# Decayed attention and two MLPs on one core: two heads' first score tiles put into one, and one read over two PSUM banks

## The chip, the core and the metric

The kernel runs on one core of a Trainium2 chip. TensorE (PE) multiplies matrices into PSUM; VectorE (DVE) and ScalarE (ACT) read PSUM and work on SBUF; GpSimd (POOL) fills and reduces small things; SyncE (SP) issues nearly all DMAs. The metric is the time of one execution in microseconds of the device, as the median of several.

## The reference

Four batches of eight heads, 576 positions, 64 features a head; then two MLPs over the 2304 tokens.

```python
scores = q @ k.T / 8
cum = cumsum(log(clip(f, 1e-4, 1)))            # f: batch, head, position
scores = where(causal, scores + cum_q - cum_k, -1e9)
attn = exp(scores - max); attn = attn / (sum(attn) + 1e-9)
x = (attn @ v)                                  # heads side by side: 2304 x 512
h = x @ w_in;  y = maximum(0.01 * h, h) @ w_out # 512 -> 2048 -> 512
g = y @ w_gate; out = (silu(g) * (y @ w_val)) @ w_out2   # 512 -> 1536 -> 512
```

All is fp32 outside. Inside, most products are taken as three half-precision products of high and low parts.

## The kernel before

**Units.** Each batch is cut into two units of queries (`UNITS`, L467): u = 0 has queries 0 to 319 (below: a 320-query unit), u = 1 queries 320 to 575 (a 256-query unit). The query tiles of 128 rows are shifted by half a tile (`hw` = 64), so that tile i holds queries 128 i - 64 to 128 i + 63. Tile 0 thus has 64 rows that nobody uses. `KW` (L469) has the width in keys of each tile: 128, 256 and 320 for u = 0, 448 and 576 for u = 1.

**Attention of a unit** (`attention`, L891). For each of four pairs of heads, and each head: `prep_head` (L721) loads q and k into `xf`, and makes `ta` and `tb` from it (rounded part, rest, and four rows of the decay, `cum`, that SP loads into `tb`); `ta` and `tb` have two buffers each. Then `exps` (L757) for each tile: two matmuls, from `tb` and `ta`, of at least 256 columns into a PSUM bank; `exp_of` (L744) with one VectorE instruction that scales, adds the mask, writes SBUF and takes the extreme of each row; and one exponential on ScalarE that sums the row too. The 576-key tile doesn't fit in a bank of 512 floats: it is two halves of 288 in two banks and two VectorE instructions, the second of which goes on from the first one's extreme. `probs` (L788) cuts the normalised tile into a high part (ScalarE) and a low part (VectorE) in `ph`, one DMA transposes both into `pt`, and some tiles later `pv` (L798) multiplies with V, two heads at a time on the two column halves of the array, and cuts the result into `xs_buf`. GpSimd clears the parts of `ph` that no tile writes. In batch 0 the scores need one matmul each; its 320-query unit has a form of its own (`attention_f32`, L820), which uses widths 64, 192 and 320 already.

**Work around it.** While a unit's attention runs, the first MLP (`moe_h`, `moe_y`) of the unit before is multiplied (`along`, L1350), which needs that unit's `xs_buf`. From the second unit of batch 1 on, `rate` (L1386) also spreads 36 places among the score tiles: `place` (L946) loads a block of second-MLP weights (512 KB, as 8-byte words), turns it into floats on VectorE, and stores it (256 KB). A last stage (`gate_val`, L1209, `out_stage`) does the second MLP over all tokens with Strassen-like products; three banks of `pp_ring` (L1148) serve a block.

**PSUM.** Eight banks: `ps_s` (three, scores), `ps_x` (one, PV), `ps_m` (four, first MLP); `ps_r`, `pp_ring` and `po_ring` use some of them again.

**Order.** Nothing runs as written: a `Plan` (L84) records all operations, estimates each duration (`cost`), draws an order for the five queues by lists with due times in 120 rounds and takes the one with the least simulated end (`emit`, L382). Each queue then runs its part in that order, and a waiting instruction holds what is behind it. All instructions so have the line of a helper, L415.

Of the kernel before, what the change touches and what calls it, by code (L numbers as in the profile page):

```python
# [9 lines left out]
F32 = mybir.dt.float32  # L10
# [11 lines left out]
P = 128  # L22
# [61 lines left out]
class Plan:  # L84
# [17 lines left out]
    def record(self, eng, method, args, kw):  # L102
        outs = [kw[k] for k in self.OUT if kw.get(k) is not None]
        ins = [x for k, x in kw.items() if k not in self.OUT and isinstance(x, bass.AP)]
        pos = [x for x in args if isinstance(x, bass.AP)]
        if pos and not kw.get("out"):
            outs.append(pos[0])
            pos = pos[1:]
        ins += pos
        dur, nbytes = self.cost(eng.name, method, outs, ins, self.pairs)  # L110
        fn = getattr(eng.real, method)
        if self.group is not None:
            op = self.group
            assert op.eng in (None, eng.name)
            op.eng = eng.name
            op.dur += dur
            op.calls.append((fn, args, kw))
        else:
            op = self.new(eng.name)
            op.dur = dur  # L120
            op.bytes = nbytes
            op.calls.append((fn, args, kw))
        op.reads += [(x.tensor.name,) + spans(x) for x in ins]

        op.writes += [(x.tensor.name,) + (spans(x) if x.space != PSUM else ((0, P), [(0, 2048)])) for x in outs]
        if self.group is None:
            self.close(op)
# [320 lines left out]
def body(ctx, tc, qk, v, f, w_in, w_out, w_gate, w_val, w_out2, out):  # L448
# [19 lines left out]
    KEYS = [q0 + nq for q0, nq, _ in UNITS]  # L468
    KW = [[max(i * P + hw, min(i + 1, 2) * P) for i in tiles] for _, _, tiles in UNITS]  # L469
    W = qk.shape[3]  # L470
# [22 lines left out]
    psp = ctx.enter_context(tc.tile_pool(name="ps", bufs=1, space=PSUM))  # L493
    banks = [psp.tile([P, 512], F32, name=f"bank{i}") for i in range(8)]
    ps_s, ps_x, ps_m, ps_r = Ring(banks[:3]), Ring(banks[3:4]), Ring(banks[4:]), Ring(banks[4:7])
    a_s = Arena(pool, 1856, "smalls")
# [18 lines left out]
    for u in range(2):  # L515
        a_m.at = n
        gf_ring[u] = a_m.cut(PER[u] * UNITS[u][1], F32, (5, 3)[u])
    raw_ring = a_w.cut(RAW * 2, I32, 3)
    cv_ring = a_w.cut(RAW, I32, 1)
# [105 lines left out]
    def decay():  # L625
# [26 lines left out]
        nc.gpsimd.affine_select(out=mask[:, 4 * P:], in_=mask[:, 4 * P:], pattern=[[-1, P + hw]],  # L652
                                compare_op=ALU.is_ge, fill=NEG, base=0, channel_multiplier=1)
        csf = scr[:, 3 * S:3 * S + 4 * W].rearrange("r (a s) -> r a s", a=4)
        cs = csf.bitcast(F32R)
# [87 lines left out]

    def exp_of(tp, parts, ms, mx, total):  # L744

        for n, (ps, a, e) in enumerate(parts):
            nc.vector.tensor_tensor_reduce(
                out=tp[:, a:e], in0=ps[:, :e - a], in1=ms[:, a:e], scale=-0.125,
                scalar=(3.0e38 if n == 0 else mx[:, 1:2]), op0=ALU.add, op1=ALU.min,
                accum_out=mx[:, 0:1] if n == len(parts) - 1 else mx[:, 1:2])  # L750
        w = parts[-1][2]
        nc.scalar.activation(out=tp[:, :w], in_=tp[:, :w], func=AF.Exp, bias=mx[:, 0:1], scale=-1.0, accum_out=total)

    def mask_of(i):
        return mask[:, (4 - i) * P + hw:]

    def exps(o, n):  # L757
# [3 lines left out]
        tp = tp_ring[o.u].next()  # L761
        mx = sm(2, "mx", 8)
        if kw <= 512:
            parts = [(0, kw, max(kw, 256))]
        else:
            parts = [(0, kw // 2, kw // 2), (kw // 2, kw, kw - kw // 2)]
        pss = []
        nc.begin()
        for a, e, w in parts:
            ps = ps_s.next()  # L770
            if o.b == 0:
                nc.tensor.matmul(ps[:, :w], lhsT=o.xf[:D + 2, q:q + P],
                                 rhs=o.xf[:D + 2, o.k.start + a:o.k.start + a + w], start=True, stop=True)
            for l in range(2 if o.b else 0):
                t, k = (o.tb, D + 4) if l == 0 else (o.ta, P)
                nc.tensor.matmul(ps[:, :w], lhsT=t[:k, q:q + P], rhs=t[:k, o.k.start + a:o.k.start + a + w],
                                 start=(l == 0), stop=(l == 1))
            pss.append(ps)
        nc.done()
        exp_of(tp, [(ps, a, e) for ps, (a, e, w) in zip(pss, parts)], mask_of(i), mx, o.sums[:, n:n + 1])  # L780
        o.tp.append((tp, kw))
        if n == len(KW[o.u]) - 1:
            nc.vector.tensor_scalar(out=o.sums[:, :n + 1], in0=o.sums[:, :n + 1], scalar1=1e-9, scalar2=1.0 / PSCALE,
                                    op0=ALU.add, op1=ALU.mult)
            o.rc = sm(3, "rc", 3)
            nc.vector.reciprocal(out=o.rc[:, :n + 1], in_=o.sums[:, :n + 1])

    def probs(g, n, hi, lo):  # L788

        tp, kw = g.tp[n]  # L790
        rc = g.rc[:, n:n + 1]
# [28 lines left out]
    def attention_f32():  # L820
# [9 lines left out]
        for h in range(H + 1):  # L830
            if h < H:
# [12 lines left out]
                for ci in tiles:  # L844
                    kw, q = KW0[ci], qc + ci * P - hw
                    ps, tp, mx = ps_s.next(), tp_ring[0].next(), sm(2, "mx", 8)
                    mms(ps[:, :kw], [(xf[:D + 2, q:q + P], xf[:D + 2, kc:kc + kw], True, True)])
                    exp_of(tp, [(ps, 0, kw)], mask_of(ci), mx, sums[:, ci:ci + 1])
                    tps.append(tp)
# [41 lines left out]
    def attention(b, u):  # L891

        later, t = [], 0
        nb = NBK[u] // 2
        at_block = [(5, 0, 2), (0, 4)][u]
        rests = [(4, 10), (3, 12)][u]
        for x in ph_ring.bufs if b else ():
            for i in rests:
                nc.gpsimd.memset(x[:, i * P + hw:(i + 1) * P], 0.0)
        for hp in range(NHP):  # L900
            pts = []
            for x in range(2):
                o = prep_head(b, u, 2 * hp + x)
                for n, kw in enumerate(KW[u]):
                    if later and later[0][0] <= t:
                        pv(*later.pop(0)[1])
                    exps(o, n)
                    t += 1
                    yield kw
                ph, pt = ph_ring.next(), pt_ring[u].next()  # L910
                for n, kw in enumerate(KW[u]):
                    hi, lo = (ph[:, (l * nb + at_block[n]) * P:][:, :kw] for l in range(2))
                    probs(o, n, hi, lo)
# [3 lines left out]
            def at(x, j, l, pts=pts):  # L917
                pb = blocks(pts[x])[:, l * nb:(l + 1) * nb, :]
                if u == 0:
                    if j == 2:  # L920
                        return [(pb[:, 4:5, hw:], 256)]
                    tail = [(pb[:, j:j + 3:2, :], hw)]
                    return tail if j else [(pb[:, 5:6, hw:], 0)] + tail
                if j == 4:
# [222 lines left out]
    s_o2, i_o2 = a_s.cut(1, F32), a_s.cut(1, F32)  # L1147
    pp_ring, po_ring = Ring(banks[:6]), Ring(banks[6:])  # L1148

# [235 lines left out]
    gv_places = chain(*(stage_gv(n) for n in range(NB2)), stage_o2())  # L1385
    rate = (4 * NB2 + NF2) / (sum(H * len(UNITS[u][2]) for _, u in todo) - 24)  # L1386
    for b, u in todo:
# [80 lines left out]
```

## Time and profile before

| | |
|---|---|
| median of three runs | 922.84 us (922.84 to 923.4) |
| profiled execution | 925.66 us, its span 923.9 us |
| mean granted TensorE clock | 0.998 |
| TensorE busy | 98% of the span |
| VectorE, ScalarE, GpSimd busy | 86%, 73%, 5% |

The span goes from the first to the last instruction of the profiled execution. The names on the left of an arrow are what an instruction writes, those on the right what it reads: `att_bytes` is the memory of the attention (`xf`, tiles, `ph`, `pt`), `wi_bytes` and `wo_bytes` that of weights, `moe_bytes` and `g_bytes` that of the first MLP, `smalls` holds numbers for each row, `bank` is PSUM. In the timeline, instructions of one kind that follow each other are one row, and "us" is from the first one's start to the last one's end; matmuls overlap.

### The profile page before, as it was taken

To read this page: it belongs to the slowest core of one execution; us is meant where nothing else is said; L and a number is where in the kernel's file an instruction comes from. 1 tells how busy PE (TensorE), PEld (TensorE's weight loads), DVE (VectorE), ACT (ScalarE), POOL (GpSimd) and SP (SyncE) were. 2 spreads that over 40 slices of the span, in tenths; PEclk is the share of its full clock that TensorE was granted. 3 is DMA by queue.
4 is the path that set the end of the run, shared out by engine and by line. 5 is a ranking of instruction groups with operands and counts; after the bars stand their busy time and mean duration, and the time that the engine had idled before them with its cause. 6 is when DMAs were issued, how large, how long until landed. Compare 5 with 4: busy or idle time off the path is not lost.

```text
span 923.9 us, 25387 instructions
## 1 busy us (share of the span) xinstructions
PE 908.8 (98%) x10018; PEld 776.7 (84%) x10018; DVE 794.1 (86%) x2078; ACT 676.1 (73%) x1665; POOL 45.4 (5%) x119
## 2 busy tenths in 40 slices
PE   9999999999999999899999999999999999999998
PEld 5666678877688777788778899999999999999997
DVE  7999999988899999799788999986778695968685
ACT  8886689988689887688886878774647474755553
POOL 3410000000000010000000000000000000000000
PEclk9999999999999999999999999999999999999999
DMA  7568985797999999989867452110101000100001
GB/s 229 179 202 217 271 212 115 187 248 172 259 270 259 255 263 229 298 249 254 188 147 191 140 178 96 64 59 20 37 18 31 25 25 25 37 25 2 26 6 42
DMA packets 163431, 132.81 MB, mean 144 GB/s; under 512 B 117432, under 2 KB 130752, under 8 KB 163280
## 3 DMA queue, kind: packets, MB, share of 16 engines
q1 hardware_dynamic: 163312, 131.20, 53.5%
q8 instruction: 78, 1.28, 0.6%
q14 instruction: 41, 0.34, 0.1%
HBM read 79.99 MB, written 22.83 MB: 111 GB/s over the span
## 4 chain that ended last, share of the span: by engine, by line
PE 58%; DVE 7%; DMA 3%; ACT 3%; issue 1%; POOL 0%; SPq 0%; ACTq 0%; DVEq 0%; POOLq 0%
PE bank L415 58%; DVE att_bytes L415 2%; DVE stage L415 1%; DVE wo_bytes L415 1%; ACT att_bytes L415 1%; DMA tb<-out_dram 1%; ACT moe_bytes L415 1%; DMA att_bytes<-att_bytes 1%; DVE smalls L415 1%; DVE wi_bytes L415 1%; DMA att_bytes<-in_qk_dram 1%; DMA gate_val_dram<-wo_bytes 1%; DVE g_bytes L415 1%; DVE tb L415 0%; DVE ta L415 0%
## 5 line engine op out<-in xcount | busy, mean ns | idle before, releaser
L415 PEld LDWEIGHTS <-att_bytes 128*128 128x128 f16 (+1 forms) x4062 | 233.8, 100 | 18.3 <-issue 14.7
L415 PEld LDWEIGHTS <-wi_bytes 128*128 128x128 f16 x2292 | 192.2, 98 | 42.4 <-issue 3.1
L415 PE MATMUL bank<-g_bytes,wo_bytes 128*128 128x256 f16 (+2 forms) x1472 | 209.7, 299 | 0.0
L415 PE MATMUL bank<-moe_bytes,wi_bytes 128*128 128x320 f16 (+1 forms) x1536 | 194.5, 286 | 1.5 <-ACT moe_bytes L415 1.5
L415 ACT ACTIVATE att_bytes<-att_bytes,smalls 128x320 f32<-128x320 f32 (+11 forms) x308 | 173.7, 591 | 30.1 <-DVE smalls L415 25.5
L415 PEld LDWEIGHTS <-wo_bytes 128*128 128x128 f16 x1344 | 128.1, 98 | 33.5 <-issue 1.8
L415 DVE TENSOR_TENSOR wi_bytes<-bank,wi_bytes 128x256 f32<-128x256 f32 x270 | 109.4, 418 | 45.0 <-PE bank L415 43.6
L415 PEld LDWEIGHTS <-g_bytes 128*128 128x128 f16 x1620 | 125.9, 98 | 9.0
L415 ACT ACTIVATE wi_bytes<-wi_bytes,smalls 128x256 f32<-128x256 f32 (+2 forms) x129 | 69.9, 555 | 44.9 <-DVE wi_bytes L415 42.4
L415 PE MATMUL bank<-wi_bytes,att_bytes 128*128 128x128 f16 x1680 | 98.7, 219 | 0.5 <-ACT wi_bytes L415 0.3
L415 DVE SCALAR_TENSOR_TENSOR att_bytes<-att_bytes,smalls 128x576 f16<-128x576 f32 (+5 forms) x148 | 86.8, 614 | 4.1 <-ACT att_bytes L415 3.7
L415 PE MATMUL bank<-stage,att_bytes 128*128 128x128 f16 (+1 forms) x1389 | 86.7, 221 | 0.6 <-DVE wi_bytes L415 0.6
L415 ACT COPY wi_bytes<-bank 128x256 f32<-128x256 f32 x108 | 38.4, 363 | 51.8 <-PE bank L415 47.6
L415 DVE CUSTOM_DVE_ANT_0 att_bytes<-bank,att_bytes 128x320 f32<-128x320 f32 (+5 forms) x160 | 67.7, 441 | 7.2 <-PE bank L415 7.1
L415 POOL PARTITION_ALL_REDUCE smalls<-smalls x54 | 28.2, 523 | 757.1 <-DVE smalls L415 718.3
L415 PE MATMUL bank<-att_bytes 128*64 128x256 f16 (+4 forms) x828 | 55.5, 262 | 5.5 <-DMA att_bytes<-att_bytes 5.2
L415 ACT ACTIVATE wi_bytes<-wo_bytes 128x256 bf16<-128x256 f32 x108 | 44.0, 410 | 19.2 <-DVE wo_bytes L415 19.2
L415 PE MATMUL bank<-wo_bytes,g_bytes 128*128 128x256 f16 x432 | 55.0, 273 | 0.0
L415 DVE TENSOR_TENSOR g_bytes<-moe_bytes,g_bytes 128x320 f16<-128x320 f32 (+1 forms) x80 | 44.6, 564 | 8.2 <-ACT g_bytes L415 7.8
L415 PE MATMUL bank<-tb 68*128 68x256 f32 (+3 forms) x144 | 49.9, 360 | 1.7 <-ACT att_bytes L415 1.1
L415 DVE SCALAR_TENSOR_TENSOR stage<-stage 128x512 int32<-128x512 int32 x68 | 46.5, 684 | 0.2
L415 DVE SCALAR_TENSOR_TENSOR wo_bytes<-wi_bytes,smalls 128x512 f32<-128x512 f32 x54 | 40.1, 743 | 6.3 <-ACT wi_bytes L415 6.3
(123 smaller groups left out, 1380.1 us busy)
## 6 DMA issues: line engine op xcount, KB each, us to landing
stage<-in_moe_w_out_dram SPq DMA_DIRECT2D x28, 512.0 KB
att_bytes<-in_qk_dram SPq DMA_DIRECT2D x24, 416.0 KB
stage<-in_moe_w_in_dram SPq DMA_DIRECT2D x16, 512.0 KB
att_bytes<-in_qk_dram SPq DMA_DIRECT2D x24, 320.0 KB
stage<-in_moe_w_gate_dram SPq DMA_DIRECT2D x12, 512.0 KB
stage<-in_moe_w_val_dram SPq DMA_DIRECT2D x12, 512.0 KB
stage<-gate_val_dram SPq DMA_DIRECT2D x12, 512.0 KB
ta<-y_dram SPq DMA_DIRECT2D x18, 256.0 KB
```

The costliest lines, as they stand in the source:

```text
L415: fn(*args, **kw)
```

## The change

The first score tiles of a pair of heads share one tile of 64 keys: `exps_two` puts queries 0 to 63 of the one head on PSUM rows 0 to 63 and those of the other on rows 64 to 127, with four fp32 matmuls of 64 columns, two terms for each head, on the two column halves. It runs when the second head is prepared; its probabilities go into the second head's `ph`, and the first head's transpose has 10 blocks in place of 12. The second tiles are 192 keys wide, with matmuls of 256 columns as before. The 576-key tile lies in `two`, a tile over two banks, 288 columns on either side of the border, and one VectorE instruction reads it. A 320-query unit has 20 score tiles for 24. The banks are dealt anew: scores of a unit alternate between one bank and `two`; the last stage has five product banks for six. `rate` is worked out from the smaller number of tiles.

```diff
-        op.reads += [(x.tensor.name,) + spans(x) for x in ins]
-        op.writes += [(x.tensor.name,) + (spans(x) if x.space != PSUM else ((0, P), [(0, 2048)])) for x in outs]
+        bank = (0, P), [(0, 4096)]
+        op.reads += [(x.tensor.name,) + (spans(x) if x.space != PSUM else bank) for x in ins]
+        op.writes += [(x.tensor.name,) + (spans(x) if x.space != PSUM else bank) for x in outs]
...
-    KW = [[max(i * P + hw, min(i + 1, 2) * P) for i in tiles] for _, _, tiles in UNITS]
+    KW = [[i * P + hw for i in tiles] for _, _, tiles in UNITS]
...
-    banks = [psp.tile([P, 512], F32, name=f"bank{i}") for i in range(8)]
-    ps_s, ps_x, ps_m, ps_r = Ring(banks[:3]), Ring(banks[3:4]), Ring(banks[4:]), Ring(banks[4:7])
+    banks = [psp.tile([P, 512], F32, name=f"bank{i}") for i in range(6)]
+    two = psp.tile([P, 2 * 512], F32, name="banks")
+    ps_x, ps_m, ps_r = Ring(banks[1:2]), Ring(banks[2:]), Ring(banks[1:4])
+    ps_s, ps_f = Ring([banks[0], two]), Ring([banks[0], two, banks[4]])
...
+    mask2 = a_s.cut(hw, BF16)
...
+        for x in range(2):
+            r = slice(x * hw, (x + 1) * hw)
+            nc.scalar.copy(out=mask2[r, :], in_=mask[r, 4 * P + x * hw:4 * P + (x + 1) * hw])
...
-    def exp_of(tp, parts, ms, mx, total):
-        for n, (ps, a, e) in enumerate(parts):
-            nc.vector.tensor_tensor_reduce(
-                out=tp[:, a:e], in0=ps[:, :e - a], in1=ms[:, a:e], scale=-0.125,
-                scalar=(3.0e38 if n == 0 else mx[:, 1:2]), op0=ALU.add, op1=ALU.min,
-                accum_out=mx[:, 0:1] if n == len(parts) - 1 else mx[:, 1:2])
-        w = parts[-1][2]
-        nc.scalar.activation(out=tp[:, :w], in_=tp[:, :w], func=AF.Exp, bias=mx[:, 0:1], scale=-1.0, accum_out=total)
+    def exp_of(tp, ps, ms, mx, total):
+        nc.vector.tensor_tensor_reduce(out=tp, in0=ps, in1=ms[:, :tp.shape[1]], scale=-0.125, scalar=3.0e38,
+                                       op0=ALU.add, op1=ALU.min, accum_out=mx)
+        nc.scalar.activation(out=tp, in_=tp, func=AF.Exp, bias=mx, scale=-1.0, accum_out=total)
...
+    def exps_two(two):
+        b, kw = two[1], KW[0][0]
+        ps, tp, mx = ps_s.next(), tp_ring[0].next(), sm(1, "mx", 8)
+        nc.begin()
+        nc.pairs = True
+        for l in range(2):
+            for x, e in enumerate(two):
+                t, k = (e.tb, D + 4) if l == 0 else (e.ta, P)
+                t = t.bitcast(F32)
+                nc.tensor.matmul(ps[x * hw:(x + 1) * hw, :kw], lhsT=t[:k, e.q.start:e.q.start + hw],
+                                 rhs=t[:k, e.k.start:e.k.start + kw], start=(l == 0), stop=(l == 1))
+        nc.done()
+        nc.pairs = False
+        exp_of(tp[:, :kw], ps[:, :kw], mask2, mx, b.sums[:, :1])
+        b.tp.append((tp, kw))
...
-        mx = sm(2, "mx", 8)
-        if kw <= 512:
-            parts = [(0, kw, max(kw, 256))]
-        else:
-            parts = [(0, kw // 2, kw // 2), (kw // 2, kw, kw - kw // 2)]
-        pss = []
+        mx = sm(1, "mx", 8)
+        to = two if kw > 512 else ps_s.next()
+        if kw > 512:
+            ps_s.n += 1
+            assert ps_s.n % 2 == 0
+        c = 0 if kw <= 512 else 512 - kw // 2
         nc.begin()
-        for a, e, w in parts:
-            ps = ps_s.next()
+        for a, w in ((0, max(kw, 256)),) if kw <= 512 else ((0, kw // 2), (kw // 2, kw // 2)):
+            ps = to[:, c + a:]
...
-        exp_of(tp, [(ps, a, e) for ps, (a, e, w) in zip(pss, parts)], mask_of(i), mx, o.sums[:, n:n + 1])
+        exp_of(tp[:, :kw], to[:, c:c + kw], mask_of(i), mx, o.sums[:, n:n + 1])
         o.tp.append((tp, kw))
         if n == len(KW[o.u]) - 1:
...
-        tp, kw = g.tp[n]
+        tp, kw = g.tp[n - len(KW[g.u])]
...
-                    ps, tp, mx = ps_s.next(), tp_ring[0].next(), sm(2, "mx", 8)
+                    ps, tp, mx = ps_f.next(), tp_ring[0].next(), sm(1, "mx", 8)
...
-        nb = NBK[u] // 2
         at_block = [(5, 0, 2), (0, 4)][u]
-        rests = [(4, 10), (3, 12)][u]
-        for x in ph_ring.bufs if b else ():
+        nbs = [(5, 6), (9, 9)][u]
+        rests = [(4, 1, 5), (3,)][u]
+        assert ph_ring.n % 2 == 0
+        for x, nb in zip(ph_ring.bufs, nbs) if b else ():
             for i in rests:
-                nc.gpsimd.memset(x[:, i * P + hw:(i + 1) * P], 0.0)
+                for l in range(2) if i < nb else ():
+                    nc.gpsimd.memset(x[:, (l * nb + i) * P + hw:(l * nb + i + 1) * P], 0.0)
         for hp in range(NHP):
-            pts = []
+            pts, os = [], []
             for x in range(2):
                 o = prep_head(b, u, 2 * hp + x)
+                os.append(o)
+                nb, skip = nbs[x], (u, x) == (0, 0)
                 for n, kw in enumerate(KW[u]):
+                    if n == 0 and skip:
+                        continue
                     if later and later[0][0] <= t:
                         pv(*later.pop(0)[1])
-                    exps(o, n)
+                    if n == 0 and u == 0:
+                        exps_two(os)
+                        kw = 2 * kw
+                    else:
+                        exps(o, n)
                     t += 1
                     yield kw
...
-                pb = blocks(pts[x])[:, l * nb:(l + 1) * nb, :]
+                pb = blocks(pts[x])[:, l * nbs[x]:(l + 1) * nbs[x], :]
                 if u == 0:
                     if j == 2:
                         return [(pb[:, 4:5, hw:], 256)]
                     tail = [(pb[:, j:j + 3:2, :], hw)]
-                    return tail if j else [(pb[:, 5:6, hw:], 0)] + tail
+                    p0 = blocks(pts[1])[:, l * nbs[1] + 5:l * nbs[1] + 6, x * hw:(x + 1) * hw]
+                    return tail if j else [(p0, 0)] + tail
...
-    pp_ring, po_ring = Ring(banks[:6]), Ring(banks[6:])
+    pp_ring, po_ring = Ring(banks[:4] + [two[:, :512]]), Ring(banks[4:])
...
-    rate = (4 * NB2 + NF2) / (sum(H * len(UNITS[u][2]) for _, u in todo) - 24)
+    rate = (4 * NB2 + NF2) / (sum(H * len(UNITS[u][2]) - (0 if u else NHP) for _, u in todo) - 24)
```

## Rows read from the trace of the kernel before

**Rows 1.** The page, part 1: busy us (share of the span) xinstructions.

```profile
PE 908.8 (98%) x10018; PEld 776.7 (84%) x10018; DVE 794.1 (86%) x2078; ACT 676.1 (73%) x1665; POOL 45.4 (5%) x119
```

**Rows 2.** Waits of TensorE, whole span: us in total, times, longest us.

```profile
PE bank L415 <- DMA att_bytes<-att_bytes: 5.2, 3, 2.3
...
PE bank L415 <- ACT moe_bytes L415: 1.5, 3, 0.7
PE bank L415 <- ACT att_bytes L415: 1.1, 1, 1.1
PE bank L415 <- DVE smalls L415: 0.8, 2, 0.5
```

**Rows 3.** Windows: a 320-query unit, a 256-query unit, the last stage.

```profile
core 0: us, PE busy (x) PEld busy (x) DVE busy (x) ACT busy (x) POOL busy (x), PEclk, DMA share, GB/s
120.00:188.00 68.00, 66.88 (x637) 57.57 (x636) 64.28 (x194) 63.07 (x156) 3.65 (x12) 1.00 0.72 173
188.00:253.00 65.00, 63.38 (x523) 46.85 (x523) 56.64 (x164) 50.41 (x117) 3.98 (x13) 1.00 0.92 222
575.00:924.00 349.00, 345.76 (x5106) 332.59 (x5105) 267.84 (x578) 204.17 (x525) 6.39 (x15) 1.00 0.09 29
```

**Rows 4.** Timeline of TensorE at three unit ends: start, us, [idle before].

```profile
110.64 1.06 PE L415 MATMUL bank<-att_bytes 128*64 128x256 f16 x16 [1.26 <-DMA att_bytes<-att_bytes]
...
252.31 0.95 PE L415 MATMUL bank<-att_bytes 128*64 128x256 f16 x14 [1.62 <-DMA att_bytes<-att_bytes]
...
374.68 1.63 PE L415 MATMUL bank<-att_bytes 128*64 128x256 f16 x24 [2.35 <-DMA att_bytes<-att_bytes]
```

**Rows 5.** Window behind the third unit end, columns as in rows 3.

```profile
374.70:380.00 5.30, 5.30 (x46) 3.98 (x46) 3.53 (x14) 4.10 (x12) 0.32 (x3) 0.68 1.00 312
```

**Rows 6.** Timeline of TensorE around single tiles of first scores.

```profile
151.58 4.11 PE L415 MATMUL bank<-moe_bytes,wi_bytes 128*128 128x256 f16 x36
...
155.65 0.28 PE L415 MATMUL bank<-ta 128*128 128x256 f32 x1
155.77 1.48 PE L415 MATMUL bank<-g_bytes,wo_bytes 128*128 128x256 f16 x12
...
157.33 0.39 PE L415 MATMUL bank<-g_bytes,wo_bytes 128*128 128x256 f16 x2
```

**Rows 7.** Timeline of TensorE, matmuls on halves of the array.

```profile
45.84 0.33 PE L415 MATMUL bank<-att_bytes,g_bytes 64*64 64x64 f32 x4
...
46.10 0.64 PE L415 MATMUL bank<-att_bytes 66*128 66x448 f32 x1
...
146.34 0.93 PE L415 MATMUL bank<-moe_bytes,wi_bytes 128*128 128x256 f16 x7
147.19 0.33 PE L415 MATMUL bank<-att_bytes 128*64 128x64 f16 x4
```

**Rows 8.** Groups by form, VectorE: busy us, mean ns | idle.

```profile
L415 DVE CUSTOM_DVE_ANT_0 att_bytes<-bank,att_bytes 128x448 f32<-128x448 f32 x32 | 19.7, 615 | 1.6 <-PE bank L415 1.6
...
L415 DVE CUSTOM_DVE_ANT_0 att_bytes<-bank,att_bytes,smalls 128x288 f32<-128x288 f32 x32 | 16.4, 511 | 0.5
...
L415 DVE DVE_READ_ACCUMULATOR2_ANT smalls<- 128x1 f32 x192 | 15.4, 80 | 0.0
...
L415 DVE CUSTOM_DVE_ANT_0 att_bytes<-bank,att_bytes 128x288 f32<-128x288 f32 x32 | 14.4, 449 | 1.1 <-PE bank L415 1.0
...
L415 DVE SCALAR_TENSOR_TENSOR att_bytes<-att_bytes,smalls 128x128 f16<-128x128 f32 x24 | 8.2, 341 | 0.0
...
L415 DVE CUSTOM_DVE_ANT_0 att_bytes<-bank,att_bytes 128x128 f32<-128x128 f32 x24 | 6.6, 277 | 1.1 <-PE bank L415 1.1
```

**Rows 9.** Groups by form, ScalarE's exponentials, columns as in rows 8.

```profile
L415 ACT ACTIVATE att_bytes<-att_bytes,smalls 128x128 f32<-128x128 f32 x24 | 9.5, 397 | 4.1 <-DVE smalls L415 4.0
...
L415 ACT ACTIVATE att_bytes<-att_bytes,smalls 128x64 f32<-128x64 f32 x8 | 2.7, 338 | 0.0
```

**Rows 10.** SP: `cum` loads (min/median/max ns), and a transpose on the timeline.

```profile
L415 SPq DMA_DIRECT2D tb<-cum_dram x48: 261/283/1254, 100.9 to 470.0; - x48
...
367.68 4.80 SPq L415 DMA_TRANSPOSE att_bytes<-att_bytes  x1
```

More of the change, by code (lines that the diff above doesn't have):

```diff
@@ L777, in exps @@
                                  start=(l == 0), stop=(l == 1))
-            pss.append(ps)
         nc.done()
-        exp_of(tp, [(ps, a, e) for ps, (a, e, w) in zip(pss, parts)], mask_of(i), mx, o.sums[:, n:n + 1])
+        exp_of(tp[:, :kw], to[:, c:c + kw], mask_of(i), mx, o.sums[:, n:n + 1])
         o.tp.append((tp, kw))
         if n == len(KW[o.u]) - 1:
-            nc.vector.tensor_scalar(out=o.sums[:, :n + 1], in0=o.sums[:, :n + 1], scalar1=1e-9, scalar2=1.0 / PSCALE,
+            m = n + 1 - len(o.tp)
+            nc.vector.tensor_scalar(out=o.sums[:, m:n + 1], in0=o.sums[:, m:n + 1], scalar1=1e-9, scalar2=1.0 / PSCALE,
                                     op0=ALU.add, op1=ALU.mult)
             o.rc = sm(3, "rc", 3)
-            nc.vector.reciprocal(out=o.rc[:, :n + 1], in_=o.sums[:, :n + 1])
+            nc.vector.reciprocal(out=o.rc[:, m:n + 1], in_=o.sums[:, m:n + 1])
     def probs(g, n, hi, lo):
-        tp, kw = g.tp[n]
+        tp, kw = g.tp[n - len(KW[g.u])]
         rc = g.rc[:, n:n + 1]
@@ L845, in attention_f32 @@
                     kw, q = KW0[ci], qc + ci * P - hw
-                    ps, tp, mx = ps_s.next(), tp_ring[0].next(), sm(2, "mx", 8)
+                    ps, tp, mx = ps_f.next(), tp_ring[0].next(), sm(1, "mx", 8)
                     mms(ps[:, :kw], [(xf[:D + 2, q:q + P], xf[:D + 2, kc:kc + kw], True, True)])
-                    exp_of(tp, [(ps, 0, kw)], mask_of(ci), mx, sums[:, ci:ci + 1])
+                    exp_of(tp[:, :kw], ps[:, :kw], mask_of(ci), mx, sums[:, ci:ci + 1])
                     tps.append(tp)
@@ L911, in attention @@
                 for n, kw in enumerate(KW[u]):
+                    if n == 0 and skip:
+                        continue
                     hi, lo = (ph[:, (l * nb + at_block[n]) * P:][:, :kw] for l in range(2))
```

## The prediction

> **What bounds the kernel now.** First the page: TensorE is busy 908.8 of 923.9 us, VectorE 794.1, ScalarE 676.1 [rows 1]. So TensorE is the bound, and the change can gain in two ways only: shorter TensorE work, or fewer TensorE waits. The view of the waits, for TensorE alone, shows how little the second can be: 5.2 us for transposed probabilities (three waits), 1.5 for ScalarE's `moe_bytes` (the attention output cut for the next matmuls), 1.1 for ScalarE's `att_bytes`, 0.8 for VectorE [rows 2], 8.6 in all. The windows show why these waits stand in the attention: while the 320-query unit of batch 1 runs, VectorE is busy 64.28 of 68 us, in the 256-query unit after it 56.64 of 65; in the last stage, without attention, TensorE works 345.76 of 349 us [rows 3]. The three waits for transposes all close a 256-query unit, those of batches 0, 1 and 2: 1.26, 1.62 and 2.35 us [rows 4]. After the longest the granted clock is 0.68 over 5.3 us (partly at the lower of the two levels, 1.2 GHz); that lost another 5.3 x 0.32 = 1.7 us [rows 5]. In reach of the change, outside TensorE's own work, are thus 8.6 + 1.7 = 10.3 us.
>
> **TensorE's own work.** Before, a pair of heads has two tiles of first scores, each two matmuls of 256 columns (`max(kw, 256)` in `exps`). 36 half-precision matmuls and one such tile take 155.77 - 151.58 = 4.19 us, 12 and one tile 157.33 - 155.77 = 1.56 [rows 6]; the difference gives 0.1096 a matmul, and so 0.245 a tile, 0.49 a pair. After, it is four fp32 matmuls of 64 columns, two by two on halves of the array. The nearest row is the end of an fp32 PV group: four 64-column matmuls on halves, 46.10 - 45.84 = 0.26 with the way back to full width; the way in is 147.19 - (146.34 + 7 x 0.1096) = 0.08 [rows 7]. 0.34 in place of 0.49 for 12 pairs (batches 1 to 3): -1.8 us. Bounds: without the way in 0.26 (-2.8 us); if the halves do not overlap, since the new contraction is 68 and 128 rows and not 64, 0.08 + 2 x 0.26 = 0.60 (+1.3 us).
>
> A rule speaks against this part. A full-width matmul of 256 columns takes 0.28 us where the next starts 0.12 us later [rows 6], so about 0.16 is still in flight. The Trainium skill (TensorEngine Tiling (Array Packing), Key Properties) says that a change of tiling mode drains the engine. A whole drain on the way in would make a pair 0.26 + 0.16 = 0.42 and this part -0.8 us in place of -1.8; the sum below would be 918.8, inside the forecast's own range, and I give it a tenth of the forecast's chance. The trace has 0.08 for the way in, half of that drain, and I take the row.
>
> The 192-key tiles still have 256 matmul columns, the 576-key tiles still two matmuls of 288 for each term, and PV has as many matmuls of the same sizes: nothing.
>
> **VectorE and ScalarE.** A score read costs 615 ns for 448 columns, 449 for 288, hence 1.04 a column, and 80 for the accumulator read behind it [rows 8]. Nothing in the trace reads over two banks. Extrapolated, 576 columns take 615 + 128 x 1.04 = 748, and with 80 it is 0.83 us against 449 + 511 + 160 = 1.12: 0.29 less a tile. Bounds: none of it (the second bank costs what the second instruction did), or 0.29 + the 0.06 between 511 and 449. I take 0.29: one start, one accumulator read and one pointer fewer. For 32 tiles 9.3 us, 2.3 a 256-query unit. In a pair of first tiles two reads of 277 + 80 become one of 277 - 66 + 80 = 291: 0.42; two low parts of 341 become one of 275: 0.41; the 192-key tiles save 64 columns in two reads and two low parts: 0.27. Together 1.1 a pair, 4.4 a 320-query unit, 13.2 in three. ScalarE's exponentials go from two of 397 to one of 338 [rows 9], and its high parts and accumulator reads fall likewise: by estimate over 1 us a pair. VectorE's 64.28 of 68 us becomes about 59.9, 88% for 95%.
>
> None of this is on the path by itself; it counts where a chain of attention ends late. The 256-query units get part back: `rate` goes from 36/72 to 36/64, so that batches 1 and 2 stage 9 and not 8 weight places in such a unit. One place (`place`, for the gate and value weights) moves 512 KB in and 256 KB out; at the 222 GB/s of that stretch [rows 3] 3.5 us of transfers. There I count the gain in VectorE and the place against each other. Batch 0's unit has no places and keeps its 2.3 us, more than the 1.26 that it waits.
>
> So I let go: the waits for ScalarE and VectorE, 1.5 + 1.1 + 0.8 = 3.4 [rows 2], and the 1.26 of batch 0's end. The other two waits for transposes and the clock's 1.7 stay.
>
> **What the change adds.** The shared tile needs both heads' `ta` and `tb`, two buffers each. So the first head's are held until the second is prepared, and between the shared tile and the next pair stand two score tiles, not three. Then SP must load the `cum` rows into `tb` (median 0.28 us of issue, longest 1.25), behind transposes that hold SP up to 4.80 us [rows 10]. If the load comes late, the score matmul waits at the head of TensorE's queue, and every matmul behind it. First scores and 192- and 320-key tiles also have two PSUM places in turn, not three. Bounds for both together: nothing, or the 0.5 us of the longest wait for VectorE [rows 2] in each of 12 pairs, 6 us. I take a quarter, 1.5: a pair has 68 / 4 = 17 us [rows 3], and the median issue is far from the longest.
>
> At nothing: GpSimd clears 42 pieces and not 24, but it is busy 45.4 us in all [rows 1]; two small ScalarE copies for `mask2` lie in the start; half of 24 transposes have 10 blocks and not 12, too little on a queue that waits in order. The last stage has five product banks for six: each block takes three, and the third is the one its neighbour finished with two products earlier; TensorE's 345.76 of 349 us leave no wait to grow. If that cover were gone, a wait for ScalarE's copy would come in up to 54 blocks.
>
> **Sum.** -1.8 - 3.4 - 1.3 + 1.5 = -5.0 us. The profiled execution took 925.66 us (span 923.9, 1.8 around it) and becomes 920.7; it stands 2.8 above the median of 922.84, which becomes **917.8**. "Faster" is under 921.0, "slower" over 924.7: 0.2% is about what a measurement of this kernel can tell from no change.
>
> **Rivals.**
> 1. *The waits only move.* The order of all queues is drawn anew; the ends of attention are set by SP's queue and transfers, not by VectorE. For it: at 367.68 a transpose holds SP 4.80 us [rows 10], and its wait is the longest. Against: VectorE's 95%. Only TensorE's -1.8 is left: 921.0. Chance 0.15.
> 2. *The ends come in time too.* VectorE's relief carries through the units: 3.4 + 5.2 + 1.7 + 1.8 = 12.1 less: 910.7. Against: SP's order. Chance 0.11.
> 3. *Slower: the ninth place.* In the 256-query units of batches 1 and 2 the last transposes land 3.5 us later: 7.0, and batch 1's wait of 1.62 passes the 2.35 after which the clock fell: 1.7 more. With the forecast's gains -5.0 + 8.7 = +3.7: 926.5. It decides from 5.0 us on; below 0.7 us an end it only eats gain. For it: these are the units that wait for transposes. Against: a place has no fixed date and can be drawn elsewhere. Chance 0.14.
> 4. *Buffers held.* The 6 us bound of the shared tile in place of 1.5: -0.5, 922.3. Against: 17 us a pair. Chance 0.08.
>
> That the change does not do what it says: the two-bank read could cost as two. That takes 9.3 us from VectorE's relief, nothing from TensorE's work, and ends in rival 1.
>
> **How the numbers follow.** The forecast has 0.52, its own range 914 to 921 (PE bounds -2.8 to +1.3, new waits 0 to 6 at a quarter). Faster: 0.48 of it, all of rival 2, half of rival 1: 0.66. Same: 0.04, half of rival 1, half of rival 4, 0.02 of rival 3: 0.18. Slower: 0.16. The range 912 to 926 leaves out rival 2's lower part and what lies above rival 3's place.
>
> **What the profile after would show.** VectorE: 32 reads of 128x576 near 750 ns, the 288 forms gone, 148 score reads for 192 and 148 accumulator reads for 192. TensorE: groups of four 64-column matmuls on halves, 0.34 us with their switches. Waits of TensorE: those for VectorE and ScalarE under 2 us in all, those for transposes near 4. Wrong would be: waits for `ta` or `tb` loads in the 320-query units (rival 4), unit ends over 2.4 us with a lower clock behind them (rival 3), or the waits' sum unchanged at 8 to 9 us (rival 1).

## The result, and the profile after

The changed kernel takes 931.82 us (median of four runs, 928.8 to 932.34), the kernel before, run beside it, 923.12 (922.84 to 923.92): ratio 1.0082, interval 1.0062 to 1.0101. It is slower by about 7.6 us by that ratio (the medians lie 8.7 apart); the forecast was 917.8, the range ended at 926. The profiled execution, 928.8 us at a mean granted clock of 1.00, is the fastest of the four; the other three stand at 931.5 to 932.3 with 0.992 and 0.993. Part of the loss in those three is thus the clock; where it fell can't be seen, since they have no trace.

The page of the changed kernel, part 1, against [rows 1]:

```profile
span 927.1 us, 25356 instructions
PE 905.7 (98%) x10059; PEld 773.4 (83%) x10063; DVE 779.9 (84%) x1978; ACT 664.5 (72%) x1632; POOL 53.4 (6%) x137
```

VectorE and ScalarE have become shorter by 14.2 and 11.6 us, TensorE's busy time by 3.1 (1.7 of it is the clock fall of [rows 5], which this execution doesn't have). But the span less TensorE's busy time, its idle time, went from 923.9 - 908.8 = 15.1 to 21.4. So the relief arrived, and TensorE waits longer all the same. VectorE's groups by form show that the new instructions cost what [rows 8] gave (748 forecast for the first):

```profile
L415 DVE CUSTOM_DVE_ANT_0 att_bytes<-banks,att_bytes 128x576 f32<-128x576 f32 x32 | 24.0, 751 | 1.5 <-PE banks L415 1.4
L415 DVE DVE_READ_ACCUMULATOR2_ANT smalls<- 128x1 f32 x148 | 12.0, 81 | 0.0
...
L415 DVE CUSTOM_DVE_ANT_0 att_bytes<-banks,att_bytes 128x192 f32<-128x192 f32 x20 | 7.0, 350 | 0.3
L415 DVE CUSTOM_DVE_ANT_0 att_bytes<-bank,att_bytes 128x192 f32<-128x192 f32 x12 | 4.2, 346 | 0.0
```

The waits of TensorE, columns as in [rows 2]:

```profile
PE bank L415 <- DMA att_bytes<-att_bytes: 4.0, 5, 1.6
PE bank L415 <- DVE smalls L415: 1.8, 3, 0.8
PE banks L415 <- issue: 1.8, 1, 1.8
PE bank L415 <- ACT moe_bytes L415: 1.6, 1, 1.6
PE banks L415 <- DVE smalls L415: 1.6, 3, 0.8
...
PE banks L415 <- DMA g_bytes<-in_qk_dram: 1.5, 1, 1.5
PE bank L415 <- issue: 1.3, 1, 1.3
PE bank L415 <- DVE wi_bytes L415: 1.1, 1, 1.1
```

The waits for transposes fell from 5.2 to 4.0, as forecast, and at the ends of the units of batches 1 and 2 they are shorter than in [rows 4]:

```profile
250.96 0.60 PE L415 MATMUL bank<-att_bytes 128*64 128x256 f16 x7 [0.51 <-DMA att_bytes<-att_bytes]
...
381.05 0.60 PE L415 MATMUL bank<-att_bytes 128*64 128x256 f16 x7 [1.60 <-DMA att_bytes<-att_bytes]
```

What is new are score matmuls that wait for VectorE: the two lines with `smalls`, all but one wait of 0.77 us in the MLP (`smalls` holds the row's extreme, so this is VectorE's read of a score place), and, by their place in time, the two with `issue`. In all, score matmuls waited 0.8 us for VectorE's reads in the kernel before (the last line of [rows 2]) and wait 5.7 here. The timelines of VectorE and TensorE at two of them:

```profile
172.74 0.48 DVE L415 CUSTOM_DVE_ANT_0 att_bytes<-bank,att_bytes 128x320 f32<-128x320 f32 x1
...
173.29 0.39 PE L415 MATMUL bank<-tb 68*128 68x256 f32 x1 [0.78 <-DVE smalls L415]
...
358.79 2.21 DVE L415 SCALAR_TENSOR_TENSOR att_bytes<-att_bytes,smalls 128x640 f16<-128x640 f32 x3
360.91 0.75 DVE L415 CUSTOM_DVE_ANT_0 att_bytes<-banks,att_bytes 128x576 f32<-128x576 f32 x1
...
361.77 0.37 PE L415 MATMUL banks<-tb 68*128 68x288 f32 x1 [1.76 <-issue]
```

A read ends at 172.74 + 0.48 = 173.22 or 360.91 + 0.75 = 361.66, and the matmul that goes into the same place starts 0.07 and 0.11 later. The first is in a 320-query unit, where two places alternate. The second is in a 256-query unit, where before and after a 448-key and a 576-key tile come back to their own places from head to head: no place was taken away there. The wait comes from where the instructions stand in their queues: VectorE has three others to do (2.21 us) before it comes to the read. That place is not this order's alone. In the further orders below the profiled executions of the changed kernel show a score wait of 1.23, 1.50, 1.92 and 1.32 us there (draws a to d, 359 to 365 us; none in e, nor in a second execution of a), and none of the six of the kernel before has one.

The windows over the stretches of [rows 3]:

```profile
120.00:188.00 68.00, 65.46 (x640) 55.27 (x637) 58.33 (x174) 56.92 (x138) 4.16 (x19) 1.00 0.73 170
188.00:253.00 65.00, 64.49 (x542) 48.03 (x542) 56.22 (x151) 53.30 (x123) 4.63 (x17) 1.00 0.89 218
575.00:924.00 349.00, 348.41 (x5144) 334.65 (x5140) 270.98 (x585) 206.90 (x532) 8.14 (x15) 1.00 0.10 30
```

VectorE is down to 58.33 of 68 us in the 320-query unit (59.9 forecast), yet TensorE is busy 65.46 there and was 66.88. The last stage, with five product banks, has hardly more waits than before: 0.5 us from 575 us on, 0.6 before; counted from its first products on, at about 540 us, 1.6 us against 1.0.

### The profile page after: what moved, and what is told of

It is laid out like the page before. It is cut to its first block, busy times and chain, and to the rows that moved or that the text cites. A ratio compares the mean times of both kernels' runs of the same rounds, so it can differ in the third digit from the quotient of the medians.

```text
span 927.1 us, 25356 instructions
## 1 busy us (share of the span) xinstructions
PE 905.7 (98%) x10059; PEld 773.4 (83%) x10063; DVE 779.9 (84%) x1978; ACT 664.5 (72%) x1632; POOL 53.4 (6%) x137
## 4 chain that ended last, share of the span: by engine, by line
PE 65%; DVE 18%; DMA 9%; ACT 4%; issue 3%; POOL 1%; SPq 0%; DVEq 0%; ACTq 0%; POOLq 0%
PE bank L415 59%; PE banks L415 6%; DVE att_bytes L415 6%; DMA att_bytes<-att_bytes 4%; DVE stage L415 3%; DVE wi_bytes L415 2%; DVE wo_bytes L415 2%; DVE smalls L415 2%; DMA stage<-in_moe_w_gate_dram 1%; ACT att_bytes L415 1%; DVE tb L415 1%; DVE ta L415 1%; DMA stage<-in_moe_w_out_dram 1%; DVE g_bytes L415 1%; DMA att_bytes<-in_v_dram 1%
## 5 line engine op out<-in xcount | busy, mean ns | idle before, releaser
L415 ACT ACTIVATE att_bytes<-att_bytes,smalls 128x192 f16<-128x192 f32 (+10 forms) x284 | 161.3, 593 | 40.8 <-DVE smalls L415 33.1
L415 DVE TENSOR_TENSOR wi_bytes<-bank,wi_bytes 128x256 f32<-128x256 f32 x217 | 89.1, 420 | 34.9 <-PE bank L415 33.8
L415 DVE SCALAR_TENSOR_TENSOR att_bytes<-att_bytes,smalls 128x576 f16<-128x576 f32 (+5 forms) x136 | 80.1, 622 | 7.6 <-ACT att_bytes L415 7.3
L415 PE MATMUL bank<-wi_bytes,att_bytes 128*128 128x128 f16 x1344 | 83.1, 219 | 1.1 <-DVE wi_bytes L415 1.1
L415 POOL PARTITION_ALL_REDUCE smalls<-smalls x54 | 34.0, 630 | 733.2 <-DVE smalls L415 731.8
L415 PE MATMUL bank<-stage,att_bytes 128*128 128x128 f16 (+1 forms) x1113 | 73.4, 221 | 0.3 <-ACT wi_bytes L415 0.3
L415 ACT COPY wi_bytes<-bank 128x256 f32<-128x256 f32 x86 | 30.8, 363 | 43.9 <-PE bank L415 40.5
L415 ACT ACTIVATE wi_bytes<-wo_bytes 128x256 bf16<-128x256 f32 x108 | 44.1, 411 | 17.9 <-DVE wo_bytes L415 17.7
L415 PE MATMUL bank<-att_bytes 128*64 128x256 f16 (+3 forms) x800 | 49.1, 256 | 4.3 <-DMA att_bytes<-att_bytes 4.0
L415 ACT ACTIVATE moe_bytes<-bank 128x320 f32<-128x320 f32 (+1 forms) x80 | 38.8, 491 | 10.1 <-PE bank L415 10.1
L415 DVE CUSTOM_DVE_ANT_0 att_bytes<-bank,att_bytes 128x448 f32<-128x448 f32 (+3 forms) x72 | 35.1, 489 | 10.4 <-PE bank L415 10.3
```

The costliest lines, as they stand in the source:

```text
L415: fn(*args, **kw)
```

## The experiments

Two theories stood against each other. *The change costs*: two score places, tiles held for two heads, whatever the order. *The order costs*: the planner draws all five queues anew when the operations change (80 draws, 40 for each of its two look-ahead times; the 120 told above is wrong), and how well TensorE's queue meets its inputs differs by several us from order to order. Where "its order kept" is said below, all five queues hold the same instructions in the same order, apart from the edit.

### Parts alone, in a kept order

**before_one_read.** The kernel before in its order; two of the three score banks become one two-bank tile, and one instruction reads each 576 tile.

```diff
-    banks = [psp.tile([P, 512], F32, name=f"bank{i}") for i in range(8)]
+    two = psp.tile([P, 2 * 512], F32, name="banks")
+    banks = [banks[0], two[:, :512], two[:, 512:]] + banks[1:]
...
+            b.calls = [(nc.vector.real.tensor_tensor_reduce, (), dict(
+                out=tp[:, :w], in0=two[:, 512 - w // 2:512 + w // 2], in1=ms[:, :w], ...
```

> The kernel before, every queue in exactly its order, with one thing changed: the second of the two reads of a 576-key tile is one read over two banks and the first is gone (32 tiles). Theory A (the two-bank read itself costs, or does not help): the read's row is near 960 ns, or the time rises by 1 us or more. Theory B (the read is good, the loss lies in the new order and in the dealing of the banks): the row is near 750 ns, VectorE's busy time falls by 9 us, and the time is the same or up to 2 us less, 921 to 923.5.

Measured 947.96 us, 1.0265 (1.0238 to 1.0292). The loss isn't the read's own time: its row is 750 ns. VectorE's busy time falls by 1.9 us only, not by the 9 expected (the durations added up fall by 7.4). TensorE's waits:

```profile
PE banks L419 <- DVE wi_bytes L419: 14.8, 31, 1.4
PE banks L419 <- DVE smalls L419: 3.8, 6, 1.2
PE bank L419 <- DMA att_bytes<-att_bytes: 2.5, 2, 1.4
```

Nearly all of the first line lies in the last stage, where both halves of the tile serve as product banks of their own: a matmul into one half waits until VectorE has read the other. Matched instruction by instruction with the kernel before, this one lags 3.8 us at 110 us, 2.0 at 379, 2.9 at 575, and 22 at the end. In between, the waits for transposes fall from 5.2 us [rows 2] to 2.5, that of batch 2's end from 2.35 [rows 4] to 1.13. So the read itself helps the ends of units in that order, and the joint tile hurts wherever its halves are used apart (the changed kernel uses one half in the last stage).

**after_third_place.** The changed kernel in its order; each score tile of a 320-query unit may go to any free one of three places (the lone bank, either half of the two-bank tile).

```diff
+        for t in sorted((t for t in need if not need[t]), key=first.get):
+            free = [p for p in range(3) if not any(p in q and first[o] < last[t] and first[t] < last[o]
+                                                   for o, q in taken.items())]
+            p = min(free, key=lambda p: used[p])
```

> The changed kernel, every queue in exactly its order, but in the 320-query units a score tile goes into any free one of three single banks (the lone bank and either half of the two-bank tile), where it had two places in turn. Theory A (two score places in the 320-query units make score matmuls wait for VectorE): the three waits for VectorE there (0.5, 0.8 and 0.8 us in the changed kernel's profile) go, and the time falls by 2 to 4 us against the changed kernel. Theory B (VectorE is simply late where the order wants it, and the wait moves to the next instruction): under 1 us.

Measured 928.93 us, 1.0061 (1.0036 to 1.0086), beside 1.0082 (1.0062 to 1.0101): some 2 us, with intervals that overlap. The three waits of 0.5, 0.8 and 0.8 us did go, but two others came, 1.20 and 0.90 us, of matmuls into a half of the two-bank tile, where the halves wait for each other again. So this run takes the price of two places away only to put a like one in its place, and can't say what two places cost. Most of the loss stays.

### The same operations in other orders

Five further orders of each kernel, by one constant of the planner.

```diff
-    MARGIN = 300.0
+    MARGIN = 330.0          # draw b
-LEADS = (12e3, 18e3)
+LEADS = (12.5e3, 17.5e3)    # a;  c: 11.5e3, 18.5e3;  d: 11e3, 17e3;  e: 13e3, 19e3
```

> The kernel before with one constant of the planner (MARGIN 300 to 330), which makes it draw another order of the same operations. Theory A (the loss is the change's own): within 2 us of the kernel before. Theory B (each draw of an order is worth some us by luck, and the kernel before holds a lucky one): 926 to 932.

> The changed kernel with the same planner constant (MARGIN 300 to 330), another order of the same operations. Theory A (the loss is the change's own): 929 to 933 again. Theory B (luck of the draw): anywhere from 920 to 935, and it may lie below the kernel before.

> The kernel before, another draw of the order (LEADS 12.5e3 and 17.5e3 in place of 12e3 and 18e3). Theory A (the 936 of the other draw was a bad one, the kernel before is typical): 921 to 927. Theory B (the kernel before is a lucky draw among orders that scatter by some 10 us): 928 to 938.

> The changed kernel, the same draw constants (LEADS 12.5e3 and 17.5e3). Theory A (the change itself costs some 8 us in any order): 8 us above the kernel before in the same draw. Theory B (luck of the draw; the change itself gains a little): 926 to 936, on average 0 to 5 us below the kernel before in the same draw.

> The kernel before, a third draw (LEADS 11.5e3 and 18.5e3). Theory A: 921 to 927. Theory B: 928 to 938.

> The changed kernel, the third draw (LEADS 11.5e3 and 18.5e3). Theory A: 8 us above the kernel before in the same draw. Theory B: 926 to 936, on average 0 to 5 us below it.

> The kernel before with the planner's two look-ahead settings at 11 and 17 us (12 and 18): the same operations in another order. By the theory that the order of the queues sets several us: anywhere in the 923 to 937 of the four draws so far, more likely above the kernel before, since that is the fastest of them. If the orders were worth nothing, 922 to 925.

> The changed kernel with the same settings. If the change costs some 8 us in any order, it stands 6 to 10 us above the other kernel of this pair; if its own worth is near nothing and the order's luck is some 5 us, the pair's difference lies anywhere from -7 to +7, and the mean of all pairs stays within 3 us of nothing.

> The kernel before with settings 13 and 19 us. As for the draw before: 923 to 937 if the order makes several us, 922 to 925 if not.

> The changed kernel with settings 13 and 19 us. 6 to 10 us above its partner if the change costs in any order; -7 to +7 around it if the order's luck decides.

Ratios to the kernel before, which is the left entry of the first line. "Idle" is the span less TensorE's busy time, "transposes" the line of waits `att_bytes<-att_bytes`, both of the one profiled execution, in us (before / after):

| order | before | after | after less before | idle | transposes |
|---|---|---|---|---|---|
| own | 1 | 1.0082 (1.0062 to 1.0101) | +0.0082 | 15.1 / 21.4 | 5.2 / 4.0 |
| a | 1.0028 (1.0006 to 1.0049) | 1.0005 (0.9988 to 1.0021) | -0.0023 | 17.7 / 15.3 | 5.2 / 3.0 |
| b | 1.0149 (1.0110 to 1.0189) | 1.0104 (1.0071 to 1.0137) | -0.0045 | 25.5 / 24.6 | 8.4 / 5.9 |
| c | 1.0028 (1.0007 to 1.0049) | 1.0042 (1.0026 to 1.0057) | +0.0014 | 21.1 / 18.8 | 7.0 / 6.5 |
| d | 1.0044 (1.0022 to 1.0067) | 1.0028 (1.0013 to 1.0043) | -0.0016 | 17.7 / 16.9 | 6.6 / 4.3 |
| e | 1.0032 (1.0015 to 1.0048) | 1.0047 (1.0026 to 1.0067) | +0.0015 | 15.3 / 17.7 | 2.8 / 4.1 |
| mean | 1.0047 | 1.0051 | +0.0004 | 18.7 / 19.1 | 5.9 / 4.6 |

Orders of the same operations lie up to 1.5% apart, and the kernel before has the best of its six. The six differences have a standard deviation of 0.0044, so their mean is +0.4 us with a standard error of 1.7 (0.0044 / 2.45 x 923), and a 95% interval of -3.9 to +4.7 (five degrees of freedom). A cost of 8 us in any order lies outside, and three pairs have the changed kernel ahead by the middles; the gain of 5 us that was forecast lies outside as well, though not by much. The first pair is the one that raised the question; the five drawn afterwards give -1.0 us by themselves, standard error 1.1, interval -3.9 to +1.9. Draw a taken once more (below) gave 1.0009 (0.9987 to 1.0031), so the runs repeat much better than the orders agree.

### One kernel's operations in the other's order

Every operation that both kernels have keeps its rank; new ones stand where the operations stood that they replace, and an operation moves back only where its inputs force it.

```diff
-            order = self.schedule(k % rounds == 0)
+        for d in struct.unpack("%dh" % len(self.ops), zlib.decompress(base64.b85decode("".join(ORDER)))):
+            at += d
+            order.append(self.ops[at])
```

> The changed operations in the order of the kernel before: every operation that both kernels have keeps its rank on its queue, the shared tile stands where the odd head's first tile stood, the 576 read where the second of two reads stood, and an operation moves back only as far as its inputs force it (29 of 1390 TensorE groups do). If the order makes the time (my theory), it comes to the kernel before or a little below: ratio 0.995 to 1.002, 919 to 926 us, with transposes' waits as before (5 us) and score waits under 3. If the change costs in itself (two score places, the shared tile, held tiles), it stays at the changed kernel's time: ratio 1.006 to 1.010, 929 to 933, with 5 to 7 us of waits for VectorE's reads of the score places.

> The other way round: the operations of the kernel before in the order of the changed kernel, an even head's first tile standing just ahead of where the shared tile stood. By the order theory ratio 1.005 to 1.015 (928 to 937 us: after's order, and the wider VectorE work besides). If the change costs in itself, the cost is gone: ratio 0.998 to 1.003, 921 to 926.

Measured: the changed operations in the order of before 948.22 us, 1.0257 (1.0219 to 1.0295); the operations of before in the changed kernel's order 965.08, 1.0442 (1.0411 to 1.0474). Both theories expected otherwise for each: an order is worth its time only with the operations that it was drawn for, and swapping doesn't separate order and change. But each run shows which waits its operations make where nothing is drawn around them. The changed operations in the order of before, timelines of VectorE and TensorE:

```profile
166.35 0.20 DVE L400 CUSTOM_DVE_ANT_0 att_bytes<-bank,smalls 128x64 f32<-128x64 f32 x1
166.48 0.08 DVE L400 DVE_READ_ACCUMULATOR2_ANT smalls<- 128x1 f32 x1
...
166.61 0.41 PE L400 MATMUL bank<-tb 68*128 68x320 f32 x1 [1.91 <-DVE smalls L400]
```

A third tile waits until the tile two before it, here the shared one, has been read from the same place; with three places it would not. Nine such waits of 128x320 tiles, 0.3 to 2.1 us, add up to 11.5 us. The last stage from its first products on, columns as in [rows 3], in the kernel before and in this run:

```profile
540.30:923.90 383.60, 379.25 (x5684) 365.44 (x5682) 299.15 (x657) 232.44 (x595) 7.10 (x17) 1.00 0.13 41
...
551.70:943.60 391.90, 382.38 (x5685) 366.15 (x5682) 300.56 (x657) 232.93 (x595) 7.10 (x17) 1.00 0.13 40
```

With five banks TensorE is idle for 391.90 - 382.38 = 9.5 us, against 383.60 - 379.25 = 4.4. In the changed kernel's own order the waits for two places are 0.47, 0.78 and 0.80 us, and those of the last stage 1.6: the planner drew around them, and what it drew has other waits. The other way round, the first tiles of before meet a VectorE that is busy elsewhere when their place should come free:

```profile
156.02 0.75 DVE L400 SCALAR_TENSOR_TENSOR wo_bytes<-wo_bytes,smalls 128x512 f16<-128x512 f32 x1
156.68 0.29 DVE L400 CUSTOM_DVE_ANT_0 att_bytes<-bank,att_bytes 128x128 f32<-128x128 f32 x1
...
157.03 0.58 PE L400 MATMUL bank<-tb 68*128 68x256 f32 x1 [3.29 <-DVE smalls L400]
```

### The one read and the third place in two orders

The changed kernel in its order, and then draw a of it in its order, with two reads for each 576 tile; in draw a also the third place.

```diff
+        if w > 512:
+            h, halves = w // 2, []
+            for a, c, first in ((0, 1, 3.0e38), (h, 0, mx[:, 1:2])):
+                halves.append((nc.vector.real.tensor_tensor_reduce, (), dict(
+                    out=tp[:, a:a + h], in0=ps[:, a:a + h], in1=ms[:, a:a + h], scale=-0.125, scalar=first,
```

> The changed kernel in its own order, but each 576 tile read by two instructions of 288 columns, as before (32 instructions, 32 accumulator reads and 32 pointers more, 9 to 10 us of VectorE in all, 0.29 a tile). If the one read is worth something where it stands, the ratio goes from the changed kernel's 1.008 to 1.010 to 1.014 (2 to 5 us more, above all where score matmuls wait for the read of a 576 tile and at the ends of the 256-query units). If VectorE's relief lies beside the path, 1.006 to 1.010 as the changed kernel itself.

> Draw a of the changed kernel (settings 12.5 and 17.5 us) once more, as the base for the two runs beside it: ratio 0.998 to 1.003, 922 to 926 us.

> Draw a of the changed kernel with its order kept, but the score tiles of a 320-query unit may use a third place (either bank of the two-bank tile). If two places in turn cost about 3 us in any order, as they did in the changed kernel's own, this is 2 to 4 us below draw a: ratio 0.995 to 1.000. If the places cost nothing where the order is a better one, it is within 1 us of draw a.

> Draw a of the changed kernel with its order kept, but each 576 tile read by two instructions of 288 columns. If the one read is worth about 3.5 us in any order, as it was in the changed kernel's own, this is 2 to 5 us above draw a: ratio 1.002 to 1.007. If the worth came from that order alone, it is within 1 us of draw a.

Two reads in the changed kernel's order: 935.04 us, 1.0120 (1.0086 to 1.0155), 3.5 us above 1.0082 by the middles, intervals overlapping. The trace says where, for its one execution. The timeline at one late point, and the windows behind it and behind a unit's end (the third figure from the right of a window is the granted clock):

```profile
366.32 0.58 PE L400 MATMUL banks<-tb 68*128 68x288 f32 x1 [2.45 <-issue]
```

```profile
366.30:372.90 6.60, 6.58 (x24) 4.20 (x25) 6.46 (x21) 6.60 (x16) 1.04 (x1) 0.50 1.18 184
255.70:260.50 4.80, 4.80 (x42) 3.77 (x42) 2.75 (x9) 2.50 (x7) 0.67 (x7) 0.64 0.96 305
```

This is the wait of 361.77 above: 2.45 us and not 1.76, with the clock behind it at 0.50 (the lower level) for 6.6 us. In the changed kernel the same stretch ran at full clock:

```profile
361.90:367.00 5.10, 5.10 (x37) 3.72 (x38) 4.99 (x16) 5.10 (x14) 0.00 (x0) 1.00 1.20 162
```

6.6 x 0.50 + 4.8 x 0.36 = 5.0 us of TensorE's time went to the clock at these two places in that execution, against nothing in the profiled one with one read. That one is the exception among its four, though: the other three have mean clocks of 0.992 and 0.993, those with two reads 0.989 to 0.995. So this tells where the two profiled executions part, and not what the read is worth on average.

Draw a, three kernels on one chip: unedited 924.53 us, 1.0009 (0.9987 to 1.0031); with the third place 925.54, 1.0014 (0.9995 to 1.0033); with two reads 926.42, 1.0025 (1.0008 to 1.0042). The third place gives nothing there, but again it brings waits of its own: score waits for VectorE in the 320-query units are 2.8 us with it and 0.6 in the unedited run, so what is left there to gain was small. Two reads cost 1.5 us by the middles, which these intervals don't settle. That the read's worth depends on what stands behind it in the order is likely, and not shown. None of the kernels tried is measurably faster than the kernel before.

## Why the prediction was wrong

**TensorE's own work (-1.8): mis-sized, nothing was saved.** The timeline of one shared group, after six half-precision matmuls:

```profile
159.59 0.82 PE L415 MATMUL bank<-g_bytes,wo_bytes 128*128 128x256 f16 x6
160.34 0.34 PE L415 MATMUL bank<-tb 68*64 68x64 f32 x4
160.51 0.29 PE L415 MATMUL bank<-ta 128*64 128x64 f32 x4
160.73 0.39 PE L415 MATMUL bank<-g_bytes,wo_bytes 128*128 128x256 f16 x2
```

Way in: 160.34 - (159.59 + 6 x 0.1096) = 0.09. Group and way back: 160.73 - 160.34 = 0.39. Together 0.48, where the forecast had 0.34 and the two tiles before 0.49. The groups at 285.66 and 411.30 us take 0.39 too; three that stand beside other score matmuls take 0.45 without the way in. The group is four instructions and eight records: the trace shows an fp32 matmul on halves as two. So the `x4` of [rows 7], which the forecast read as four matmuls, were two, and 0.26 was the price of half a group. The bound with 2 x 0.26 held it. Over the six orders TensorE's busy time, clock falls included, is 907.6 us before and 908.7 after on average. The way in was right (0.08 forecast). The Trainium skill's rule that a mode change drains the engine (TensorEngine Tiling (Array Packing), Key Properties) would have made the way in 0.16; the trace agrees with no more than about half of that.

**VectorE (-22.5 us in sum, 59.9 of 68): right.** 751 + 81 ns for a 576 tile; over all forms that changed, count times mean falls by 22.1 us, and the page's busy time by 14.2, since neighbouring instructions overlap in it.

**The waits let go (-3.4 and -1.3): the step that failed.** One read shortens the waits for transposes in two of three kept orders (5.2 to 2.5 us in before_one_read; 4.0 us against 5.7 with two reads in the changed kernel's order), and not in draw a (3.1 against 1.9). But the forecast took single waits of one trace, crossed them out and left all others in place. The planner keeps no place. ScalarE's `moe_bytes` wait came back as one of 1.6 us at another point, batch 0's end fell from 1.26 to 0.54 and a load in the same unit made TensorE wait 1.5. In the profiled execution the forecast wanted 3.2 us less idle time (-3.4 - 1.3 + 1.5), and there is 6.3 more: score matmuls that wait for VectorE +4.9, loads in batch 0 +1.8, transposes -1.2, the rest +0.8. Over six orders the waits for transposes fall by 1.2 us on average, and TensorE's idle time doesn't (18.7 and 19.1), though VectorE is 11.7 to 14.5 us shorter in each.

**New waits (+1.5, bounds 0 to 6): about right in size, wrong in place.** Not the held `ta` and `tb`: in the profiled execution no TensorE wait for their loads stands in a 320-query unit, and over the six orders one does, of 0.36 us (draw b). Nor, on average, the two places. In the own order they make 0.47 + 0.78 + 0.80 = 2.05 us, but over the six orders score matmuls in the 320-query units of batches 1 to 3 wait 1.7 us in all for VectorE with two places and 1.7 with three. Score waits for VectorE as a whole (releasers `DVE smalls` and `issue`, gaps over 0.15 us) do grow, from 2.5 to 4.4 us on average, and 1.3 of the 1.9 us stand in the 256-query units of batches 1 to 3 (0.3 before, 1.6 after), where the forecast saw only relief; the rest in batch 0.

**At nothing: the five banks** cost next to nothing in the drawn orders (waits in the last stage of 0.8 us before and 0.9 after, on average over six), and 5 us more idle time in the order of before. The cover named (TensorE's full last stage) was not what held it; the new order was. GpSimd's busy time is 53.4 us for 45.4, and TensorE's waits for it 2.2 us for 2.1.

**Rival 3** (the ninth place) isn't seen: the ends of the 256-query units of batches 1 and 2 waited 0.51 and 1.60 us, less than 1.62 and 2.35 [rows 4]. That the ninth place has a part in the new waits in the middle of these units is not excluded: no run kept `rate` as it was. **Rival 4**'s half on places is part of the own order's loss. **Rival 1** said that the order is drawn anew, and priced this at nothing: the same waits, elsewhere. That a new order of these operations can cost 3 to 14 us, and that the kernel before has the best order of the six tried, is what the range of 912 to 926 had no room for.

The change's own worth, over six orders, is +0.4 us, standard error 1.7: the forecast's -5.0 less the 1.8 that wasn't there and less most of the 4.7 of waits. By the middles, 7 of the 7.6 us measured are what the drawn orders of this one pair make; the interval leaves the change itself up to 4.7 of them. Which choice of the order costs most stays open: no run changed the order at one place alone, and none took the shared tile alone.

## What to carry to other kernels

Where a planner draws the order from the operations, every edit is two changes, and the second is a draw: time several orders of both kernels before a difference under 1.5% is put down to the edit, and forecast the spread of the orders with it. Test a part in a kept order, then in a second one, since what a shorter instruction gave in one order (3.5 us by the middles) was 1.5 in the next. Before a row's price is used, count its records against the instructions in the code.

## What the runs showed of the hardware

- One VectorE instruction over two PSUM banks costs as one over one bank: 751 ns for 576 columns, against 617 for 448 columns: 1.05 a column more, as between 350 (192 columns) and 617.
- Four fp32 matmuls of 64 columns on halves (eight records) take as long, 0.48 us with the ways in and back, as four of 256 columns in the rounded form at full width (2 x 0.245).
- A TensorE wait of 1.76 us left the granted clock at 1.00; one of 2.45 at the same point was followed by 6.6 us at 0.50. The length of the wait alone doesn't decide: 2.06 us there was followed by 3.4 us at 0.50 (after_third_place), and 2.62 at a unit's end left the clock at 1.00 (the kernel before in draw a, at 377.68 us).
- Two halves of one PSUM tile, used apart, cost some 30 waits of half a microsecond in one stage (14.8 us in 31): a matmul into one half stood until the other had been read. Whether the engines or the program's semaphores ask for that was not tried.
